# An adaLN block on one core: the start of the k projection rearranged in depth blocks

## The chip, the cores and the metric

The kernel runs on one core of a Trainium2 chip. The metric is the device time of one execution in microseconds (us). Five queues of instructions run beside each other and each keeps its order: TensorE (PE, with its weight loads PEld), VectorE (DVE), ScalarE (ACT), GpSimd (POOL) and SyncE (SP), which issues the transfers. They wait for each other through semaphores.

## The reference

One sequence of 2048 tokens of width 512 goes through two halves, each modulated by a condition vector `c`. All arrays are fp32.

```python
mod = (silu(c) @ w_mod).reshape(1, 6, 1, 512)
sa, ca, ga, sb, cb, gb = mod[:, 0], ..., mod[:, 5]
h = layernorm(x) * (1 + ca) + sa
q, k, v = split(h @ wqkv)                # 32 heads of 16
pq, pk = phi(q), phi(k)                  # phi(t) = where(t > 0, t + 1, exp(t)) + 1e-6
kv = einsum("bhsd,bhse->bhde", pk, v)
z = einsum("bhsd->bhd", pk)
o = einsum("bhqd,bhde->bhqe", pq, kv) / (einsum("bhqd,bhd->bhq", pq, z) + 1e-6)
x = x + ga * (o @ wo)
h = layernorm(x) * (1 + cb) + sb
x = x + gb * (((h @ w_gate) * (h @ w_up)) @ w_down)      # inner width 1376
```

## The kernel before

The tokens are worked in four chunks of 512, each of four token tiles of 128 (`NT` = 16 tiles, `i` counts them). The width of 512 is four depth blocks of 128. Products keep fp32 accuracy by splitting each operand into a high part, rounded for TensorE, and a low remainder: ScalarE copies the high part (`split`, L183), VectorE subtracts (L184), and TensorE makes three matmuls (high by high, high by low, low by high; `product`, L192). One such triple is needed per depth block and token tile.

The order of the work is written out by hand; no scheduler changes it. Each engine takes its instructions in the order in which the Python lines emit them. There are two pools of four PSUM banks each, `ps_acc` (`acc_bank()`) and `ps_w` (`bank()`); a new tile takes a bank that is free and waits for the last reader of it. All large SBUF tiles come from one ring of 99.

The start, L341 to L389, which the change rewrites, does the following.

- `keep_on(n)` (L141) makes TensorE multiply a tile of zeros n times. Nothing reads the result.
- `Norm` (L214) holds one chunk: `stats` (VectorE, mean and variance), `rstd_of` (a small add on VectorE and a power on GpSimd), `nmr_of` (VectorE), `xhat` (ScalarE, the normalised tile), `transpose` (TensorE, L246), and `modulated` (L259), which for one depth block scales the transposed block by column `ca` and shifts it by column `sa` on ScalarE, rounds it to the high part (VectorE when `cast` is given, otherwise a second ScalarE pass) and subtracts on VectorE.
- The columns `ca` and `sa` of the modulation are accumulated on VectorE (`mod_acc`), summed over partitions by four one-column matmuls into one bank (`mod_col`, L163) and copied out by VectorE in one instruction (`col_out`, L169).
- The weights of k are split one block at a time (`split_raw`), in turn with `modulated` of the same block.
- Token tiles 0 and 1 are then projected together, block by block (`product2`, L200), into two accumulating banks; tiles 2 and 3 follow one after the other (`proj`, L282).
- The second chunk is normalised meanwhile: its statistics for four tiles, one power, then `xhat` on ScalarE.

Phi of k is computed by `k_phi` (two ScalarE passes and one VectorE pass) and split by `k_split` (kh on ScalarE, kl on VectorE); the normalised tile is split by `k_split_x`. `t_tile` multiplies the two into four banks that accumulate over all 16 tiles. The loop over the tiles (L421) mixes for each tile `i`: the projection of tile `i + 2`, the splits of tile `i + 1`, the transposes and scalings of the next chunk in its first two tiles, `k_phi` of tile `i + 2`, and `t_tile(i)`. The dictionary `extra` (L405) adds other work behind a tile: the four splits of the q weights stand behind tiles 0, 1 and 2. `q_at` (L419) puts the first q projection at tile 3.

Of the kernel before, what the change touches and what calls it, by code (L numbers as in the profile page):

```python
# [22 lines left out]
def tile_adaln_block(  # L23
# [12 lines left out]
    nc = tc.nc  # L36
# [3 lines left out]
    KD = D // P  # L40
    NJ = 4
    CH = NJ * P
    NCH = S // CH
# [16 lines left out]
    consts = pool("consts", 1)  # L60
# [10 lines left out]
    def T(p, tag, shape=(P, D), dt=F32, bufs=None):  # L71
        cnt[0] += 1
        return p.tile(list(shape), dt, tag="t" if p is tiles else tag, name=f"{tag}_{cnt[0]}", bufs=bufs)

    def B(tag, shape=(P, D), dt=F32):

        return T(tiles, tag, shape, dt)

    def acc_bank():
        return T(ps_acc, "acc")  # L80

    def bank():
        return T(ps_w, "bank")
# [6 lines left out]
    ones = consts.tile([P, P], F32, name="ones")  # L90
# [28 lines left out]
    def load_qkv(n):  # L119
        return [load(wqkv_v[k, :, n * D:(n + 1) * D], "raw") for k in range(KD)]  # L120
# [6 lines left out]
    raw_k = load_qkv(1)  # L127
    xts.append(load_x(1))
    raw_q = load_qkv(0)
    raw_v = load_qkv(2)  # L130
# [10 lines left out]
    def keep_on(n):  # L141
        for _ in range(n):
            nc.tensor.matmul(ps_idle, idle[:, :P], idle, start=True, stop=True)
# [19 lines left out]
    def mod_col(acc, ps):  # L163

        for b in range(KD):
            nc.tensor.matmul(ps[:, b:b + 1], acc[:, b * P:(b + 1) * P], ones[:, 0:1], start=True, stop=True)
        return ps

    def col_out(v, ps, add):  # L169
        t = consts.tile([P, KD], F32, name=f"col{v}")  # L170
        nc.vector.tensor_scalar(t, ps[:, :KD], add, None, op0=ALU.add)
        return t
# [9 lines left out]
    def split(src, h, l, low=None):  # L182
        nc.scalar.activation(h, src, AF.Copy)  # L183
        (low or nc.vector).tensor_tensor(l, src, f32(h), op=ALU.subtract)  # L184

    def split_raw(raw, shape=(P, D), low=None):
        h = B("w", shape, F32R)
        l = B("w", shape, F32R)
        split(raw, h[:raw.shape[0]], l[:raw.shape[0]], low)
        return h, l  # L190

    def product(ps, pairs):  # L192

        n = len(pairs)
        for i, ((ah, al), (bh, bl)) in enumerate(pairs):
            nc.tensor.matmul(ps, ah, bh, start=i == 0, stop=False)  # L196
            nc.tensor.matmul(ps, ah, bl, start=False, stop=False)  # L197
            nc.tensor.matmul(ps, al, bh, start=False, stop=i == n - 1)  # L198

    def product2(pss, pairs):  # L200

        n = len(pairs[0])
        for i in range(n):
            for ps, p in zip(pss, pairs):
                (ah, al), (bh, bl) = p[i]
                nc.tensor.matmul(ps, ah, bh, start=i == 0, stop=False)
                nc.tensor.matmul(ps, ah, bl, start=False, stop=False)
                nc.tensor.matmul(ps, al, bh, start=False, stop=i == n - 1)

    def cut(pair, a, b):  # L210
        return pair[0][:, a:b], pair[1][:, a:b]


    class Norm:  # L214
# [25 lines left out]
        def xhat(self, *js):  # L240
            for j in js:
                self.n[j] = B("n")
                nc.scalar.activation(self.n[j], self.tiles[j], AF.Identity,  # L243
                                     scale=self.rstd[:, j:j + 1], bias=self.nmr[:, j:j + 1])

        def transpose(self, *ks):  # L246
            for k in ks:
                ps = turn_bank[0]()
                for j in range(NJ):
                    nc.tensor.transpose(ps[:, j * P:(j + 1) * P], self.n[j][:, k * P:(k + 1) * P], ident)  # L250
                self.ps[k] = ps
# [63 lines left out]
    def k_split(i):  # L315
        h, l = B("kh", dt=F32R), B("kl", dt=F32R)
        phi = phk[i]
        nc.scalar.activation(h, phi, AF.Identity, bias=eps_phi)
        nc.vector.scalar_tensor_tensor(l, phi, EPS_PHI, f32(h), op0=ALU.add, op1=ALU.subtract)
        kx[i] += [h, l]  # L320

    def t_tile(i, *ks):
        xh, xl, kh, kl = kx[i]
        first, last = i == 0, i == NT - 1
        for k in ks:
            a, b = k * P, (k + 1) * P
            nc.tensor.matmul(tacc[k], xh[:, a:b], kh, start=first, stop=False)  # L327
            nc.tensor.matmul(tacc[k], xl[:, a:b], kh, start=False, stop=False)  # L328
            nc.tensor.matmul(tacc[k], xh[:, a:b], kl, start=False, stop=last)  # L329
# [11 lines left out]
    n0 = norm[0]  # L341
    acc_ca, acc_sa = B("f"), B("f")
# [20 lines left out]
    mod_acc(acc_sa, raw_sa, [0, 1, 2, 3])  # L363
    ca = col_out(1, ps_ca, 1.0)
    keep_on(4)
    ps_sa = mod_col(acc_sa, acc_bank())
    keep_on(9)
    wk.append(split_raw(raw_k[0]))
    sa = col_out(0, ps_sa, 0.0)
    nx = Norm(xts[1])  # L370
    nx.stats(0)
    n0.modulated(ca, sa, 0, cast=nc.vector)
    wk.append(split_raw(raw_k[1]))
    n0.modulated(ca, sa, 1, cast=nc.vector)
    wk.append(split_raw(raw_k[2]))
    n0.modulated(ca, sa, 2)
    nx.stats(1)
    wk.append(split_raw(raw_k[3]))
    n0.modulated(ca, sa, 3)
    ps0, ps1 = acc_bank(), acc_bank()  # L380
    product2((ps0, ps1), [[(cut(n0.t[k], j * P, (j + 1) * P), wk[k]) for k in range(KD)] for j in range(2)])
    nx.stats(2, 3)
    nx.rstd_of()
    k_split_x(0)
    k_phi(0, ps0)
    nx.nmr_of()
    k_phi(1, ps1)
    k_split(0)
    nx.xhat(0, 1)  # L389

    tacc = [acc_bank() for _ in range(KD)]
    rows, cols = {}, {}
# [7 lines left out]
    def mod_part(v, *ks):  # L400
        if 0 in ks:
            accs[v] = B("f")
        mod_acc(accs[v], raw_m[v], ks)

    extra = {0: lambda: (wq.extend(split_raw(r) for r in raw_q[0:1]),),  # L405
             1: lambda: (wq.extend(split_raw(r) for r in raw_q[1:2]),),
             2: lambda: (wq.extend(split_raw(r) for r in raw_q[2:4]),),
             4: lambda: (wv.extend(split_raw(r) for r in raw_v[0:1]),),
             5: lambda: (wv.extend(split_raw(r) for r in raw_v[1:2]),),
             6: lambda: (wv.extend(split_raw(r) for r in raw_v[2:3]), mod_load(2),),  # L410
             7: lambda: (wv.extend(split_raw(r) for r in raw_v[3:4]),),
# [5 lines left out]
             13: lambda: (mod_part(5, 0, 1, 2), cols.update({4: col_out(4, mod_col(accs[4], bank()), 1.0)})),  # L417
             14: lambda: (mod_part(5, 3), wo_s.extend(split_raw(x) for x in raw_o)), 15: lambda: rows.update({5: mod_row(5, accs[5])})}
    q_at = {3: 0, 4: 1, 6: 2, 7: 3}  # L419
    ahead = {2: proj(2, wk)}  # L420
    for i in range(NT):  # L421
        ch, j = divmod(i, NJ)
        more = ch + 1 < NCH
        if i == 0:
            ahead[3] = proj(3, wk)
        elif i > 1:
            ahead[i + 2] = proj(i + 2, wk) if i + 2 < NT else proj(i + 6 - NT, wq)
        if i in q_at:
            qps = proj(q_at[i], wq)
        if more and j == 0:  # L430
            nx.xhat(2)
        if i + 1 < NT:
            k_split_x(i + 1)
        if more and j == 0:
            nx.xhat(3)
        if i + 1 < NT:
            k_split(i + 1)
        if more and j < 2:
            t_tile(i, 0, 1)
            nx.transpose(2 * j, 2 * j + 1)  # L440
            nx.modulated(ca, sa, 2 * j, 2 * j + 1, cast=nc.vector)
            norm[ch + 1:] = [nx]
        if ch + 2 < NCH and j == 2:
            nx2 = Norm(xts[ch + 2])
            nx2.stats(0, 1)
        if ch + 2 < NCH and j == 3:
            nx = nx2
            nx.stats(2, 3)
            nx.rstd_of()
            nx.nmr_of()  # L450
            nx.xhat(0, 1)
        if i + 2 < NT:
            k_phi(i + 2, ahead.pop(i + 2))
        else:
# [12 lines left out]
        t_tile(i, *range(2 if more and j < 2 else 0, KD))  # L467
        if i in extra:
            extra[i]()
    ga, gb, sb, cb = rows[2], rows[5], cols[3], cols[4]  # L470
# [60 lines left out]
    ps = proj(6, wq)  # L531
# [12 lines left out]
    for g in range(KD):  # L544
        a, b = g * P, (g + 1) * P
# [4 lines left out]
    ps = proj(8, wq)  # L550
# [9 lines left out]
    ps = proj(9, wq)  # L560
# [460 lines left out]
    ps = proj(11, wq)  # L1021
# [176 lines left out]
```

## Time and profile before

| | us |
|---|---|
| median of 3 runs (lowest to highest) | 570.78 (569.49 to 571.22) |
| profiled execution, device time | 570.02 |
| its span, first to last instruction | 568.3 |
| first useful k product starts | 18.03 |
| first product of tile 2's projection | 24.26 |
| first matmul of `t_tile(0)` | 29.71 |
| transposes of the third chunk start | 58.00 |

All times inside the execution count from the start of the span. A row of the timeline gives start, duration, engine, line, operation, output and inputs, shape and count; in square brackets stands how long the engine was idle before it and what ended the idle time. Matmuls are pipelined: the drawn durations overlap, and the pace is read from start to start. A row with x8 covers eight records.

### The profile page before, as it was taken

What the parts mean: (1) busy time and instruction counts of PE and PEld (TensorE: products, weight loads), DVE (VectorE), ACT (ScalarE), POOL (GpSimd) and SP (SyncE); (2) the same over time, 40 slices, a digit from 0 to 9 for tenths busy, and PEclk for the clock granted to TensorE, in tenths of its full rate; (3) what the DMA queues carried; (4) which work ended last, traced back from release to release, by engine and by line L of the source; (5) the groups of instructions that cost most, each with busy time, mean ns of one, the idle gap of its engine ahead of it and who ended that gap; (6) DMA issues with size and microseconds to landing.
All of it is one profiled execution on the core that took longest, in us unless ns stands there. A gap on an engine that the chain in (4) does not pass through costs nothing.

```text
span 568.3 us, 7356 instructions
## 1 busy us (share of the span) xinstructions
PE 560.3 (99%) x2575; PEld 458.8 (81%) x2575; DVE 373.1 (66%) x614; ACT 279.8 (49%) x500; POOL 186.2 (33%) x191
## 2 busy tenths in 40 slices
PE   8999999999999999999989999999999999999997
PEld 6778888888888878878878888787888888888886
DVE  7876868868768876759767777745554434344445
ACT  3785857546456546445865545534333333334110
POOL 2000000000011300000579666665667446556200
PEclk9999999999999999999999999999999999999999
DMA  8900223302301000804208553599336012200004
GB/s 289 374 3 2 74 75 110 114 0 62 93 0 47 29 1 37 260 0 149 57 2 277 180 190 104 202 348 330 115 111 178 26 57 55 57 19 2 0 1 148
DMA packets 50309, 59.34 MB, mean 104 GB/s; under 512 B 6432, under 2 KB 27168, under 8 KB 50272
## 3 DMA queue, kind: packets, MB, share of 16 engines
q1 hardware_dynamic: 50272, 58.87, 32.1%
q8 instruction: 20, 0.33, 0.2%
q14 instruction: 17, 0.14, 0.1%
HBM read 43.12 MB, written 15.73 MB: 104 GB/s over the span
## 4 chain that ended last, share of the span: by engine, by line
PE 89%; DMA 3%; issue 2%; POOL 1%; DVE 1%; ACT 1%; SPq 1%; POOLq 0%; ACTq 0%
PE bank L838 28%; PE acc L914 6%; PE acc L915 6%; PE acc L916 6%; PE acc L614 6%; PE bank L198 5%; PE bank L196 5%; PE bank L197 5%; PE acc L329 3%; PE acc L327 3%; PE acc L328 3%; PE bank L693 2%; PE bank L691 2%; PE bank L692 2%; PE bank L250 2%
## 5 line engine op out<-in xcount | busy, mean ns | idle before, releaser
L838 PE MATMUL bank<-h,w 128*128 128x512 f32 (+1 forms) x798 | 185.5, 390 | 1.8 <-ACT bank L843 1.2
L838 PEld LDWEIGHTS bank<-h,w 128*128 128x128 f32 (+1 forms) x798 | 148.2, 186 | 35.3 <-ACT bank L843 1.7
L843 ACT ACTIVATE bank<-bank 128x512 f32<-128x512 f32 (+1 forms) x38 | 22.1, 583 | 144.8 <-PE bank L838 144.8
L678 DVE TENSOR_TENSOR x<-acc,x 128x512 f32<-128x512 f32 (+1 forms) x73 | 49.1, 684 | 49.0 <-PE acc L916 48.2
L824 POOL TENSOR_TENSOR w<-raw,w 128x256 fp32r<-128x256 f32 (+3 forms) x38 | 42.4, 1117 | 106.4 <-ACT w L817 86.4
L184 POOL TENSOR_TENSOR w<-raw,w 128x512 fp32r<-128x512 f32 (+1 forms) x25 | 34.9, 1399 | 116.0 <-DVE mv L226 87.6
L914 PE MATMUL acc<-w,kh 128*128 128x512 f32 (+2 forms) x154 | 59.6, 387 | 0.0
L915 PE MATMUL acc<-w,kh 128*128 128x512 f32 (+2 forms) x154 | 59.6, 387 | 0.0
L916 PE MATMUL acc<-w,kl 128*128 128x512 f32 (+2 forms) x154 | 59.5, 386 | 0.0
L234 POOL TENSOR_TENSOR rstd<-ve,half 128x4 f32<-128x4 f32 (+1 forms) x9 | 9.4, 1044 | 126.0 <-DVE ve L233 124.5
L184 DVE TENSOR_TENSOR kl<-u,kh 128x512 fp32r<-128x512 f32 (+1 forms) x38 | 26.8, 746 | 33.1 <-ACT kh L183 31.2
L824 POOL TENSOR_TENSOR w<-t,w 128x512 fp32r<-128x512 f32 (+1 forms) x38 | 48.4, 1293 | 0.0
L196 PE MATMUL bank<-w,h 128*128 128x512 f32 x112 | 45.0, 402 | 0.0
L198 PE MATMUL bank<-w,h 128*128 128x512 f32 x112 | 43.9, 392 | 0.0
L197 PE MATMUL bank<-w,h 128*128 128x512 f32 x112 | 43.6, 389 | 0.0
L614 PE MATMUL acc<-w,xh 128*128 128x512 f32 x120 | 38.1, 399 | 0.0
L914 PEld LDWEIGHTS acc<-w,kh 128*128 128x128 f32 (+1 forms) x154 | 28.9, 188 | 6.0
L916 PEld LDWEIGHTS acc<-w,kl 128*128 128x128 f32 (+1 forms) x154 | 28.9, 188 | 5.9
L915 PEld LDWEIGHTS acc<-w,kh 128*128 128x128 f32 (+1 forms) x154 | 28.9, 188 | 5.9
L893 DVE TENSOR_TENSOR u<-bank,u 128x512 f32<-128x512 f32 (+1 forms) x19 | 13.1, 690 | 30.0 <-PE bank L838 30.0
L243 ACT ACTIVATE n<-x,nmr,rstd 128x512 f32<-128x512 f32 x32 | 24.1, 804 | 17.2 <-DVE nmr L237 15.9
L262 ACT ACTIVATE f<-bank,col,col 128x512 f32<-128x512 f32 x28 | 20.7, 775 | 14.5 <-PE bank L250 12.4
(177 smaller groups left out, 1105.1 us busy)
## 6 DMA issues: line engine op xcount, KB each, us to landing
raw<-in_w_mod_dram SPq DMA_DIRECT2D x24, 256.0 KB, 3.7
raw<-in_B_w_down_dram SPq DMA_DIRECT2D x20, 256.0 KB, 2.9
raw<-in_B_w_gate_dram SPq DMA_DIRECT2D x36, 128.0 KB, 3.7
raw<-in_B_w_up_dram SPq DMA_DIRECT2D x36, 128.0 KB, 3.6
x<-in_A_x_dram SPq DMA_DIRECT2D x16, 256.0 KB, 5.4
kept<-f SPq DMA_DIRECT2D x16, 256.0 KB, 2.0
f<-kept SPq DMA_DIRECT2D x16, 256.0 KB, 4.8
side_s<-h SPq DMA_DIRECT2D x16, 256.0 KB, 2.6
```

What stands on the lines that cost most here:

```text
L184: (low or nc.vector).tensor_tensor(l, src, f32(h), op=ALU.subtract)
L196: nc.tensor.matmul(ps, ah, bh, start=i == 0, stop=False)
L197: nc.tensor.matmul(ps, ah, bl, start=False, stop=False)
L198: nc.tensor.matmul(ps, al, bh, start=False, stop=i == n - 1)
L243: nc.scalar.activation(self.n[j], self.tiles[j], AF.Identity, scale=self.rstd[:, j:j + 1], bias=self.nmr[:, j:j + 1])
L614: nc.tensor.matmul(yps[i], x, y, start=False, stop=k == KD - 1 and x is al, skip_group_check=True)
L678: nc.vector.tensor_tensor(xt[:, a:b], dn[j][:, a:b], xt[:, a:b], op=ALU.add)
L824: sub = lambda out, x, y: (on or nc.gpsimd).tensor_tensor(out, x, f32(y), op=ALU.subtract)
L838: mm = lambda x, y, **kw: nc.tensor.matmul(ps, x[:, k], y, skip_group_check=True, **kw)
L914: nc.tensor.matmul(ps, hh[:, a:b], dh[:n, c:d], start=i == 0, stop=False)
L915: nc.tensor.matmul(ps, hh[:, a:b], dl[:n, c:d], start=False, stop=False)
L916: nc.tensor.matmul(ps, hl[:, a:b], dh[:n, c:d], start=False, stop=i == len(hs) - 1)
```

## The change

Six things are rewritten, all between the modulation columns and token tile 3.

1. The four one-column matmuls of `sa` write two banks: the first column has a bank of its own, the other three share one. VectorE copies each column out by itself; the copy of the first stands before the first weight split's subtraction, the other three behind the first block's scaling.
2. `keep_on(9)` behind them becomes `keep_on(2)`, and `keep_on(4)` stays.
3. All four token tiles of the first chunk are projected per depth block (`k_block`) into four banks, for blocks 0 and 1. Blocks 2 and 3 follow tile by tile. `product2` goes. All four blocks are rounded on VectorE.
4. The second chunk's statistics and power are done in two halves of two tiles; `xhat` of its tiles 2 and 3 is done on VectorE in one instruction each (`xhat_on`), tiles 0 and 1 stay on ScalarE. The statistics of its first tile stand behind the scaling of block 2.
5. `k_split_x(1)`, `k_phi(1)` and `k_split(1)` stand before the loop. In the loop, the transposes and scalings of the second chunk stand at tiles 1 and 2 (before: 0 and 1), and at tile 2 they come first; `t_tile(2)` goes before the projection of tile 4.
6. The four splits of the q weights stand behind the last scaling of the second chunk, at tile 2.

```diff
-    ps_sa = mod_col(acc_sa, acc_bank())
-    keep_on(9)
-    wk.append(split_raw(raw_k[0]))
-    sa = col_out(0, ps_sa, 0.0)
+    ps_sa = [acc_bank()]
+    ps_sa += [acc_bank()] * (KD - 1)
+    sa = consts.tile([P, KD], F32, name="col0")
+    def sa_block(b):
+        nc.tensor.matmul(ps_sa[b][:, b:b + 1], acc_sa[:, b * P:(b + 1) * P], ones[:, 0:1], start=True, stop=True)
+    def sa_out(b):
+        nc.vector.tensor_scalar(sa[:, b:b + 1], ps_sa[b][:, b:b + 1], 0.0, None, op0=ALU.add)
+    def block_in(b):
+        n0.modulated(ca, sa, b, cast=nc.vector)
+    def w_in(b):
+        wk.append(split_raw(raw_k[b]))
+    for b in range(KD):
+        sa_block(b)
+    keep_on(2)
+    k_ps = [acc_bank(), acc_bank(), bank(), bank()]
+    def k_block(b, *js):
+        for j in js:
+            (hh, hl), (wh, wl) = cut(n0.t[b], j * P, (j + 1) * P), wk[b]
+            nc.tensor.matmul(k_ps[j], hh, wh, start=b == 0, stop=False)
+            nc.tensor.matmul(k_ps[j], hh, wl, start=False, stop=False)
+            nc.tensor.matmul(k_ps[j], hl, wh, start=False, stop=b == KD - 1)
+    sa_out(0)
+    w_in(0)
+    block_in(0)
+    for b in range(1, KD):
+        sa_out(b)
+    w_in(1)
+    block_in(1)
+    k_block(0, 0, 1, 2, 3)
     nx = Norm(xts[1])
+    w_in(2)
+    block_in(2)
     nx.stats(0)
-    n0.modulated(ca, sa, 0, cast=nc.vector)
-    wk.append(split_raw(raw_k[1]))
-    n0.modulated(ca, sa, 1, cast=nc.vector)
-    wk.append(split_raw(raw_k[2]))
-    n0.modulated(ca, sa, 2)
+    k_block(1, 0, 1, 2, 3)
+    w_in(3)
+    block_in(3)
     nx.stats(1)
-    wk.append(split_raw(raw_k[3]))
-    n0.modulated(ca, sa, 3)
-    ps0, ps1 = acc_bank(), acc_bank()
-    product2((ps0, ps1), [[(cut(n0.t[k], j * P, (j + 1) * P), wk[k]) for k in range(KD)] for j in range(2)])
-    nx.stats(2, 3)
-    nx.rstd_of()
+    nx.rstd_of(0, 2)
     k_split_x(0)
-    k_phi(0, ps0)
-    nx.nmr_of()
-    k_phi(1, ps1)
+    k_block(2, 0)
+    k_block(3, 0)
+    k_phi(0, k_ps[0])
+    nx.nmr_of(0, 2)
+    nx.stats(2)
     k_split(0)
+    nx.stats(3)
+    nx.rstd_of(2, 4)
+    k_block(2, 1)
+    k_block(3, 1)
+    k_split_x(1)
+    k_phi(1, k_ps[1])
     nx.xhat(0, 1)
+    nx.xhat_on(nc.vector, 2)
+    k_split(1)
+    nx.xhat_on(nc.vector, 3)
+    k_block(2, 2)
+    k_block(3, 2)
+    k_block(2, 3)
+    k_block(3, 3)
...
+        def xhat_on(self, engine, *js):
+            for j in js:
+                self.n[j] = B("n")
+                engine.tensor_scalar(self.n[j], self.tiles[j], self.mv[:, j, 0:1], self.rstd[:, j:j + 1],
+                                     op0=ALU.subtract, op1=ALU.mult)
...
+    turn_at = {4 * ch + j: (ch + 1, 2 * j, 2 * j + 1) for ch in range(1, NCH - 1) for j in range(2)}
+    turn_at.update({1: (1, 0, 1), 2: (1, 2, 3)})
     for i in range(NT):
...
+        if i == 2:
+            turn_x()
+            wq.extend(split_raw(r) for r in raw_q)
...
+        if i in turn_at and i != 2:
             t_tile(i, 0, 1)
+            done = 2
+            turn_x()
+        if i == 2:
+            t_tile(i, *range(KD))
+            done = KD
+            ahead[i + 2] = proj(i + 2, wk)
```

More of the change, by code (lines that the diff above doesn't have):

```diff
@@ L198, in product @@
             nc.tensor.matmul(ps, al, bh, start=False, stop=i == n - 1)
[L200 to L208, printed above, removed]
     def cut(pair, a, b):
@@ L403, in mod_part @@
         mod_acc(accs[v], raw_m[v], ks)
[L405 to L408, printed above, removed]
+    extra = {4: lambda: (wv.extend(split_raw(r) for r in raw_v[0:1]),),
              5: lambda: (wv.extend(split_raw(r) for r in raw_v[1:2]),),
@@ L419, in tile_adaln_block @@
     q_at = {3: 0, 4: 1, 6: 2, 7: 3}
-    ahead = {2: proj(2, wk)}
+    ahead = {2: k_ps[2], 3: k_ps[3]}
+    turn_at = {4 * ch + j: (ch + 1, 2 * j, 2 * j + 1) for ch in range(1, NCH - 1) for j in range(2)}
+    turn_at.update({1: (1, 0, 1), 2: (1, 2, 3)})
     for i in range(NT):
         ch, j = divmod(i, NJ)
[L423 to L426, printed above, removed]
+        done = 0
+        if i > 2:
             ahead[i + 2] = proj(i + 2, wk) if i + 2 < NT else proj(i + 6 - NT, wq)
@@ L429, in tile_adaln_block, with turn_x @@
             qps = proj(q_at[i], wq)
-        if more and j == 0:
+        def turn_x():
+            to, *ks = turn_at[i]
+            nx.transpose(*ks)
+            nx.modulated(ca, sa, *ks, cast=nc.vector)
+            norm[to:] = [nx]
+        fresh = i > 0 and ch + 1 < NCH and j == 0
+        if i == 2:
+            turn_x()
+            wq.extend(split_raw(r) for r in raw_q)
+        if fresh:
             nx.xhat(2)
-        if i + 1 < NT:
+        if 0 < i < NT - 1:
             k_split_x(i + 1)
-        if more and j == 0:
+        if fresh:
             nx.xhat(3)
-        if i + 1 < NT:
+        if 0 < i < NT - 1:
             k_split(i + 1)
-        if more and j < 2:
+        if i in turn_at and i != 2:
             t_tile(i, 0, 1)
-            nx.transpose(2 * j, 2 * j + 1)
-            nx.modulated(ca, sa, 2 * j, 2 * j + 1, cast=nc.vector)
-            norm[ch + 1:] = [nx]
+            done = 2
[4 more added lines that the diff above has]
+            ahead[i + 2] = proj(i + 2, wk)
         if ch + 2 < NCH and j == 2:
@@ L466, in tile_adaln_block @@
             nc.scalar.activation(zb, zps, AF.Identity, bias=eps_z)
-        t_tile(i, *range(2 if more and j < 2 else 0, KD))
+        t_tile(i, *range(done, KD))
         if i in extra:
```

## The prediction

> **What bounds the kernel now.** I read the page first, for who carries the span.
>
> ```profile
> span 568.3 us, 7356 instructions
> PE 560.3 (99%) x2575; PEld 458.8 (81%) x2575; DVE 373.1 (66%) x614; ACT 279.8 (49%) x500; POOL 186.2 (33%) x191
> PE 89%; DMA 3%; issue 2%; POOL 1%; DVE 1%; ACT 1%; SPq 1%; POOLq 0%; ACTq 0%
> ```
>
> TensorE is busy for 99% and is 89% of the chain that ended last. A change that neither adds nor removes useful matmuls can then win only where TensorE stands still or does filler. Next the stretches (start and end, length, then busy time and count of PE, PEld, DVE, ACT and POOL), to see where that is.
>
> ```profile
> 0.00:18.03 18.03, 15.53 (x70) 12.44 (x71) 13.09 (x32) 6.86 (x10) 3.52 (x15) 1.00 0.88 310
> 18.03:50.00 31.97, 31.86 (x144) 25.09 (x143) 27.80 (x55) 23.39 (x39) 1.38 (x1) 1.00 0.34 122
> 50.00:155.00 105.00, 105.00 (x506) 87.12 (x506) 79.51 (x137) 62.35 (x104) 2.01 (x2) 1.00 0.24 71
> 155.00:264.00 109.00, 109.00 (x530) 89.00 (x529) 83.22 (x143) 60.79 (x104) 11.96 (x9) 1.00 0.17 58
> ```
>
> From 50 to 264 us TensorE never rests, so what the front gains there is carried on, and the change moves nothing behind token tile 3: after it each engine's instructions stand in the same order. What follows 264 us I take to shift along, its loads being released by the work before them. The busy column hides short pauses, because a paused matmul is drawn longer; so I read single rows of TensorE, start and duration.
>
> ```profile
> 14.94 1.05 PE L166 MATMUL acc<-ones,f 128*128 128x1 f32 x8
> 15.85 2.34 PE L143 MATMUL acc<-w 128*128 128x512 f32 x9
> 18.03 0.39 PE L206 MATMUL acc<-w,h 128*128 128x512 f32 x1
> ...
> 24.26 0.40 PE L196 MATMUL bank<-w,h 128*128 128x512 f32 x1
> ...
> 29.71 0.39 PE L327 MATMUL acc<-kh,xh 128*128 128x512 f32 x1
> ...
> 36.98 0.40 PE L196 MATMUL bank<-w,h 128*128 128x512 f32 x1
> ...
> 40.27 0.39 PE L327 MATMUL acc<-kh,xh 128*128 128x512 f32 x1
> ...
> 58.00 1.04 PE L250 MATMUL bank<-ident,n 128*128 128x128 f32 x8
> ```
>
> From 24.26 to 29.71 run the 24 matmuls of tiles 2 and 3: 5.45 us, so 0.227 us each when fed. That is the ruler. The 24 of the paired tiles 0 and 1 take 18.03 to 24.26, 6.23 us: 0.78 is pause. The 12 of tile 4's projection take 36.98 to 40.27, 3.29 against 2.72: 0.57 is pause. The nine before 18.03 are filler. In the printed chain, transfers precede 19.87; but VectorE has no idle time there (rows below, back to back), so it is that queue and not a load that is late.
>
> **The change, part by part.** The feeders' rows, VectorE first:
>
> ```profile
> 16.03 0.16 DVE L171 TENSOR_SCALAR col<-acc 128x4 f32<-128x4 f32 x1 [0.47 <-PE acc L166]
> 16.34 0.70 DVE L225 BATCH_NORM_STATS2 st<-x 128x6 f32<-128x512 f32 x1
> 17.07 0.18 DVE L226 BATCH_NORM_AGGREGATE mv<-st 128x2 f32<-128x6 f32 x1
> 17.17 0.40 DVE L270 CAST h<-f 128x512 fp32r<-128x512 f32 x1
> ...
> 18.21 0.69 DVE L184 TENSOR_TENSOR w<-raw,w 128x512 fp32r<-128x512 f32 x1
> 18.81 0.42 DVE L270 CAST h<-f 128x512 fp32r<-128x512 f32 x1
> 19.26 0.69 DVE L273 TENSOR_TENSOR h<-f,h 128x512 fp32r<-128x512 f32 x1
> 19.87 0.69 DVE L184 TENSOR_TENSOR w<-raw,w 128x512 fp32r<-128x512 f32 x1
> ```
>
> ```profile
> 13.64 0.63 ACT L183 ACTIVATE w<-raw 128x512 fp32r<-128x512 f32 x1 [1.49 <-DMA raw<-in_A_wqkv_dram]
> ...
> 16.23 0.78 ACT L262 ACTIVATE f<-bank,col,col 128x512 f32<-128x512 f32 x1 [1.96 <-DVE col L171]
> ...
> 23.76 0.60 ACT L291 ACTIVATE phi<-acc 128x512 f32<-128x512 f32 x1 [1.33 <-PE acc L208]
> 24.39 0.64 ACT L292 ACTIVATE phi<-phi 128x512 f32<-128x512 f32 x1
> ...
> 25.51 0.68 DVE L295 SCALAR_TENSOR_TENSOR phi<-acc,phi 128x512 f32<-128x512 f32 x1
> ...
> 26.23 0.72 ACT L318 ACTIVATE kh<-phi,eps_phi 128x512 fp32r<-128x512 f32 x1
> ```
>
> *First column.* The four columns took eight records in 1.05 us. With a bank of its own, column 0 is complete after two records, about 15.3. Its copy (0.16) ends at 15.5 instead of 16.19, ScalarE scales until 16.3 (0.78), and the cast follows at 16.37, because the statistics that stood before it (16.34 to 17.25) have moved behind block 2. It ends at 16.77, so the first product starts at 16.8 instead of 18.03: **1.2 us won**. Seven of thirteen fillers go; they covered a wait and cost nothing now. The other three copies add 0.1 us each to VectorE.
>
> *Four tiles per block.* VectorE needs per block 0.60 (weight remainder), 0.45 (cast) and 0.61 (remainder), start to start: 1.66 us. Two tiles give TensorE 6 x 0.227 = 1.36 us per block, so it ran dry; four give 2.72. The 0.78 pause goes. In its place: the third matmul wants the remainder of block 0, which runs 16.82 to 17.5, at 17.25: 0.3 lost. Block 1 is ready at 19.7 (cast 18.6) and wanted from 19.8. Block 2 is ready at 21.4, wanted 22.5. With statistics (0.8) ahead of it, block 3 is ready at 23.8, and its remainder is wanted at 23.7: 0.1 lost. The fourth tile's bank is the one block 1 is scaled from; that read ends at 18.6, before 19.1. So 48 products end at 16.8 + 10.9 + 0.4 = 28.1 instead of 29.71: 1.6 ahead. Casting blocks 2 and 3 on VectorE takes 2 x 0.45 more there.
>
> *Phi and tile 1.* Tile 0's sum is complete at 24.2, and its chain (0.60, 0.64, 0.68, 0.72) is done by 27, ahead of 28.1. Late next is tile 1's: ScalarE's copy from 26.9, two phi steps, then the two xhat put before kh (0.80 each, row below), and kh (0.72). That is 0.63 + 0.60 + 0.64 + 1.60 + 0.72 = 4.2; neighbours in a queue overlap by 0.09 (18.21 + 0.69 against 18.81), so kh ends at 30.7 and kl (0.69) at 31.45. TensorE, at tile 1 from 30.8, wants it at 31.25: 0.2 lost.
>
> *Second chunk in halves, q weights last.* Two xhat move from ScalarE to VectorE; no row of before is this form, nearest is the product with one column:
>
> ```profile
> 11.37 0.75 DVE L161 SCALAR_TENSOR_TENSOR f<-raw,sc,f 128x512 f32<-128x512 f32 x1
> 12.04 0.48 DVE L159 TENSOR_SCALAR f<-raw,sc 128x512 f32<-128x512 f32 x1
> ```
>
> It is between 0.48 and 0.75 each; I take 0.48, as one tensor is read. The power on GpSimd goes from one call to two, idle cover on both sides. The last scalings now stand before the q splits, and the 12 matmuls of tile 2's product before tile 4's projection: 2.72 us of cover, so the 0.57 pause goes. The q splits (four of 0.60) now stand ahead of tile 3's remainders and of the next statistics; TensorE meanwhile has tile 4, 5 and q 0, 36 x 0.227 = 8.2 us. By then TensorE is 1.6 - 0.2 + 0.57 = 1.97 ahead. SP's loads keep order and count, so no transfer is moved.
>
> *What it meets next.* The third chunk's transposes at 58.00. Their last input and the queue that leads to it:
>
> ```profile
> 26.49 0.16 DVE L237 SCALAR_TENSOR_TENSOR nmr<-mv,rstd 128x4 f32<-128x4 f32 x1 [0.30 <-POOL rstd L234]
> ...
> 29.62 0.69 DVE L184 TENSOR_TENSOR xl<-n,xh 128x512 fp32r<-128x512 f32 x1 [1.77 <-ACT xh L183]
> ...
> 30.94 0.69 DVE L319 SCALAR_TENSOR_TENSOR kl<-phi,kh 128x512 fp32r<-128x512 f32 x1 [0.62 <-ACT kh L318]
> ...
> 32.53 0.43 DVE L270 CAST h<-f 128x512 fp32r<-128x512 f32 x1 [0.90 <-ACT f L262]
> ...
> 51.12 0.16 DVE L237 SCALAR_TENSOR_TENSOR nmr<-mv,rstd 128x4 f32<-128x4 f32 x1 [1.21 <-POOL rstd L234]
> ...
> 56.26 0.80 ACT L243 ACTIVATE n<-x,nmr,rstd 128x512 f32<-128x512 f32 x1
> ```
>
> The last xhat ends at 57.06; the transpose that reads it is the fourth of eight, about 58.3: 1.2 us of slack. VectorE's queue sets that xhat through nmr at 51.12. It starts 0.7 earlier and gets 2.25 us more work (casts 0.9, xhat 0.96, small ones 0.4), but of its 3.59 us of idle time (0.30 + 1.77 + 0.62 + 0.90) my walk leaves 1.6 (0.3, 0.2, 0.4, 0.4, 0.3 before casts, phi and kl): -0.7 + 2.25 - 3.59 + 1.6 = about 0.45 earlier. So TensorE may come 1.2 + 0.45 = 1.65, say **1.7 us**, earlier and not 1.97; the rest turns into a pause there. Behind it nothing changes order.
>
> **Sum.** The profiled execution took 570.02 us; less 1.7 that is 568.3. The median of the runs is 570.78, which gives 569.1. I predict the middle, 568.7. Ends: with no new pause 1.2 + 0.78 + 0.57 = 2.55 won, 567.5; if the third chunk's queue comes no earlier, 1.2 won, 568.8 to 569.6.
>
> **Rivals.** *Slower: VectorE's added work.* If VectorE idles as long as before (3.59), its queue ends 2.25 - 0.7 = 1.55 later; the slack of 1.2 doesn't cover it, and the transposes wait: 0.35 slower, 570.4 (571.1 from the median). It decides once idle time stays above 3.2 us. For it: 27.80 of 31.97 us busy already. Against: three of the four waits quoted are for ScalarE, which loses two casts and two xhat.
>
> *The column doesn't come early.* If its copy still waits for all four, the start is 0.7 later, as is the whole front: 1.0 won, 569.0 to 569.8. In the built program the semaphore stands on the first column's matmul, which speaks against.
>
> *The clock falls back.* Fewer fillers stand between 13 and 16.8 us. The trace knows a slow matmul:
>
> ```profile
> 4.71 1.91 PE L143 MATMUL acc<-w 128*128 128x512 f32 x4
> ...
> 8.01 1.32 PE L143 MATMUL acc<-w 128*128 128x512 f32 x5
> ```
>
> Four took 1.91 us, five then 1.32: over 0.4 us each, then 0.23. If the half pace returned for the six us that it lasted at first (1.99 to about 8), three us are lost: 570.02 - 1.7 + 3.0 = 571.3, or 572.1 from the median; it decides at 3.4 us of half pace. Against: the new gap is 0.3 us, and the idle time before the transposes at 10.08 did not bring it back.
>
> ```profile
> 10.08 0.66 PE L257 MATMUL bank<-ident,n 128*128 128x128 f32 x4 [0.52 <-ACT n L243]
> ```
>
> The Trainium skill's page "TensorE: Matmul & The Clock Gate" (Part 1, "What's actually happening") halves the clock only after a window of about 3.4 us without activity. By that rule the change would cost nothing here; the trace agrees as far as 0.52 us of idling goes.
>
> **Chances.** Forecast (1.3 to 2.5 won; 567.5 to 569.5) 0.68, of it 0.50 at 1.7 or more, as the ends lie 0.4 below and 0.85 above; queue no earlier, or no early column, 0.15; VectorE's work on the path 0.10; clock 0.07. About 0.3%, 1.7 us, is what a measurement can tell from no change. VectorE's and the clock's price stay inside it and pass it only when exceeded (half pace for over 6.8 us; xhat at 0.75 and the q splits late as well): 0.05 of each. So faster 0.50; within 0.18 + 0.15 + 0.05 + 0.02 = 0.40; slower 0.10. Range 567.3 to 571.0: it reaches to VectorE's price and leaves out what exceeds it and the clock.
>
> **What would show it.** First product near 16.8; no pause over 0.3 until 28.1; a pause of 0.1 to 0.4 at tile 1's kl and at the third chunk's transposes near 56.4; tile 4's projection in 2.72 us. Wrong: matmuls 0.4 apart after 16.8, or a pause over 1.5 us at the transposes.

## The result and the profile after

The changed kernel takes 567.6 us (median of 6 runs, 567.43 to 568.24); the kernel before took 570.0 us beside it (6 runs, 569.49 to 571.22). The ratio is 0.9957, 95% interval 0.9945 to 0.9969: faster by 2.4 us, 0.43%. The profiled executions, 568.24 and 570.02 us, lie 1.8 us apart.

The page of the changed kernel: span, busy times, and the chain that ended last, by engine.

```profile
span 566.5 us, 7353 instructions
PE 556.8 (98%) x2568; PEld 456.7 (81%) x2568; DVE 375.1 (66%) x622; ACT 277.0 (49%) x496; POOL 186.5 (33%) x192
PE 90%; issue 2%; ACT 2%; DMA 2%; POOL 1%; DVE 1%; SPq 1%; POOLq 0%; DVEq 0%
```

TensorE has 7 instructions fewer, the fillers, and is still what carries the span. Single rows of TensorE show where the time went; compare the prediction's rows at 18.03, 29.71, 36.98 and 58.00.

```profile
15.03 1.05 PE L367 MATMUL acc<-ones,f 128*128 128x1 f32 x8
...
17.03 0.47 PE L386 MATMUL acc<-w,h 128*128 128x512 f32 x1 [0.38 <-DVE h L266]
...
18.00 0.40 PE L386 MATMUL acc<-w,h 128*128 128x512 f32 x1
...
28.31 0.39 PE L323 MATMUL acc<-kh,xh 128*128 128x512 f32 x1
...
31.29 0.40 PE L324 MATMUL acc<-kh,xl 128*128 128x512 f32 x1
31.63 0.50 PE L325 MATMUL acc<-kl,xh 128*128 128x512 f32 x1
31.96 0.39 PE L323 MATMUL acc<-kh,xh 128*128 128x512 f32 x1
...
38.55 0.39 PE L196 MATMUL bank<-w,h 128*128 128x512 f32 x1
...
41.27 0.39 PE L196 MATMUL bank<-w,h 128*128 128x512 f32 x1
...
56.24 1.14 PE L246 MATMUL bank<-ident,n 128*128 128x128 f32 x8
57.14 0.48 PE L323 MATMUL acc<-kh,xh 128*128 128x512 f32 x1
```

The first product starts 1.00 us earlier than before, the 48 products of four tiles end 1.40 us earlier (28.31 against 29.71), tile 4's projection runs through in 2.72 us, and at the third chunk's transposes TensorE is 1.76 us ahead. They take 0.90 us to the next matmul. In the kernel before they took 0.79, which this row of it gives against 58.00:

```profile
58.79 0.47 PE L327 MATMUL acc<-kh,xh 128*128 128x512 f32 x1
```

So 0.11 us of the lead is lost there and 1.65 stays.

Places count from the start of the span, which isn't fixed to the work. The one-column matmuls of `sa` start at 15.03 here, at 14.94 in the kernel before, and between 14.60 and 15.16 in the traces below, though nothing ahead of them that they wait for was changed. For differences of tenths of a us the distance from this row is the safer measure. By it the lead is 1.09 us at the first product and 1.74 behind the transposes.

Now the changed kernel's rows of VectorE and ScalarE that feed these points.

```profile
15.45 0.16 DVE L370 TENSOR_SCALAR col<-acc 128x1 f32<-128x1 f32 x1 [0.40 <-PE acc L367]
...
16.45 0.43 DVE L266 CAST h<-f 128x512 fp32r<-128x512 f32 x1 [0.24 <-ACT f L258]
...
21.26 0.69 DVE L215 BATCH_NORM_STATS2 st<-x 128x6 f32<-128x512 f32 x1
...
30.09 0.55 DVE L239 TENSOR_SCALAR n<-x,mv,rstd 128x512 f32<-128x512 f32 x1
30.88 0.69 DVE L315 SCALAR_TENSOR_TENSOR kl<-phi,kh 128x512 fp32r<-128x512 f32 x1 [0.25 <-ACT kh L314]
...
50.61 0.16 DVE L227 SCALAR_TENSOR_TENSOR nmr<-mv,rstd 128x4 f32<-128x4 f32 x1 [1.21 <-POOL rstd L224]
...
50.81 1.52 ACT L233 ACTIVATE n<-x,nmr,rstd 128x512 f32<-128x512 f32 x2 [4.27 <-DVE nmr L227]
```

Two numbers matter for what follows. `nmr` of the third chunk starts at 50.61 instead of 51.12, and the first matmul behind the transposes starts 6.53 us after it. ScalarE, which normalises that chunk, has then waited 4.27 us for `nmr`.

### The profile page after: what moved, and what is told of

The parts are those of the page before. It is cut to its first block, busy times and chain, and to the rows that moved or that the text cites. A ratio compares the mean times of both kernels' runs of the same rounds, so it can differ in the third digit from the quotient of the medians.

```text
span 566.5 us, 7353 instructions
## 1 busy us (share of the span) xinstructions
PE 556.8 (98%) x2568; PEld 456.7 (81%) x2568; DVE 375.1 (66%) x622; ACT 277.0 (49%) x496; POOL 186.5 (33%) x192
## 4 chain that ended last, share of the span: by engine, by line
PE 90%; issue 2%; ACT 2%; DMA 2%; POOL 1%; DVE 1%; SPq 1%; POOLq 0%; DVEq 0%
PE bank L886 27%; PE acc L962 6%; PE acc L963 6%; PE acc L964 6%; PE acc L662 6%; PE bank L196 5%; PE bank L197 5%; PE bank L198 5%; PE acc L325 3%; PE acc L324 3%; PE acc L323 3%; PE bank L741 2%; PE bank L739 2%; PE bank L740 2%; PE bank L246 2%
## 5 line engine op out<-in xcount | busy, mean ns | idle before, releaser
L196 PE MATMUL bank<-w,h 128*128 128x512 f32 x104 | 41.7, 401 | 0.0
L198 PE MATMUL bank<-w,h 128*128 128x512 f32 x104 | 40.6, 390 | 0.0
L197 PE MATMUL bank<-w,h 128*128 128x512 f32 x104 | 40.5, 389 | 0.0
L233 ACT ACTIVATE n<-x,nmr,rstd 128x512 f32<-128x512 f32 x30 | 22.6, 804 | 16.0 <-DVE nmr L227 14.7
L183 ACT ACTIVATE w<-raw 128x512 fp32r<-128x512 f32 (+2 forms) x44 | 26.2, 618 | 2.5 <-DMA raw<-in_A_wqkv_dram 1.5
```

## The experiments

Each kernel was timed beside the kernel before; "won" is the median of before less the kernel's own. Medians are known to about 0.7 us (the half-width of the intervals), so smaller steps are read in the traces. Every kernel below computes the whole reference.

### The changed kernel once more

> The changed kernel, unaltered, for a second trace. Theory (TensorE's feed at the start sets the gain): against the kernel before, 1.8 us less, as in the two traces (568.3 to 566.5); first product within 0.2 of 17.03, third chunk's transposes within 0.2 of 56.24. Rival (something behind the front adds to it, since the medians differ by 2.4 and the traces by 1.8): transposes at the same place, but the stretch from 57.1 to the end over 0.4 us shorter than its 509.4.

567.96 us (567.43 to 568.67, 5 runs), 2.5 won, ratio 0.9959 (0.9946 to 0.9971). The rows of the transposes and of the last matmul, from this trace:

```profile
56.03 1.17 PE L246 MATMUL bank<-ident,n 128*128 128x128 f32 x8
...
561.84 0.28 PE L964 MATMUL acc<-w,kl 128*128 128x256 f32 x1
```

and the last matmul of the changed kernel's first trace:

```profile
562.64 0.28 PE L964 MATMUL acc<-w,kl 128*128 128x256 f32 x1
```

The two traces of one and the same kernel are 0.2 us apart at the transposes and 0.8 at the end. The 0.2 is there at the columns already (14.82 against 15.03). From the matmul behind the transposes to the end of the span this trace takes 508.7 us and the first 509.4; that difference is the sign that the rival named. But the other traces of this document take 508.7 to 509.5 there, and one 510.5, with no edit in that stretch, and the first trace is the slowest of its six executions. So whether the 0.6 us by which the traces fall short of the medians is scatter or a gain behind the front stays open.

### Two tiles per block again

```diff
-    k_block(0, 0, 1, 2, 3)
+    k_block(0, 0, 1)
...
-    k_block(1, 0, 1, 2, 3)
+    k_block(1, 0, 1)
...
-    k_block(2, 2)
-    k_block(3, 2)
-    k_block(2, 3)
-    k_block(3, 3)
+    for j in (2, 3):
+        for b in range(KD):
+            k_block(b, j)
```

> Undoes the third part alone: blocks 0 to 3 for tiles 0 and 1 only, then tile 2, then tile 3. Theory (VectorE's pace per block sets TensorE's): tile 0's last block is ready at 23.1 (cast) and 23.8 (remainder) as before, so tile 0 ends at 24.4 as in the changed kernel, but with 12 fewer matmuls done; the 12 cost 2.7 us later, less what pauses at tile 1 and the transposes took (0.2): 2.0 to 2.6 us over the changed kernel, about the time of the kernel before. Rival (only the 0.78 us pause of the kernel before comes back): 0.8 us over.

570.3 us (569.64 to 571.35, 11 runs), 0.2 won, ratio 1.0001 (0.9992 to 1.001). Rows of TensorE:

```profile
17.16 0.47 PE L386 MATMUL acc<-w,h 128*128 128x512 f32 x1 [0.38 <-DVE h L266]
...
23.28 0.50 PE L386 MATMUL acc<-w,h 128*128 128x512 f32 x1 [1.25 <-DVE h L266]
...
25.73 0.39 PE L386 MATMUL bank<-w,h 128*128 128x512 f32 x1
...
58.83 1.03 PE L246 MATMUL bank<-ident,n 128*128 128x128 f32 x8
```

Without the four tiles everything else of the change wins nothing. The 24 matmuls of tiles 0 and 1 take 8.57 us (17.16 to 25.73), so 3.12 us are pause, against 0.78 before; at block 3 TensorE stands still for 1.25 us at a stretch. VectorE needs more time per block here: from the first cast to the start of the last block's remainder its rows span 6.68 us (16.58 to 23.26) instead of 5.32 (17.17 to 22.49), and two casts of 0.45 us are the main thing that was added between them. The transposes begin 2.6 us later than in the changed kernel.

### The first column late again

Three runs take the early column apart. The first puts all four columns into one bank with one copy:

```diff
-    ps_sa = [acc_bank()]
-    ps_sa += [acc_bank()] * (KD - 1)
+    ps_sa = [acc_bank()] * KD
...
-    sa_out(0)
+    nc.vector.tensor_scalar(sa, ps_sa[0][:, :KD], 0.0, None, op0=ALU.add)
...
-    for b in range(1, KD):
-        sa_out(b)
```

> Undoes the first part alone: the four columns of sa in one bank, one copy. Theory: the copy starts about 0.7 later (after all eight records, 16.1 instead of 15.45), so do the first product (17.7) and the third chunk's transposes (56.9), because VectorE's queue starts later by the same; the time is 0.6 to 0.7 over the changed kernel. Rival (VectorE's queue to the transposes has slack and catches up): first product at 17.7, transposes within 0.3 of 56.24, under 0.3 us lost.

568.95 us (567.89 to 570.09, 9 runs), 1.5 won, ratio 0.9975 (0.9964 to 0.9986).

```profile
17.63 0.50 PE L385 MATMUL acc<-w,h 128*128 128x512 f32 x1 [0.95 <-DVE h L266]
...
56.85 1.16 PE L246 MATMUL bank<-ident,n 128*128 128x128 f32 x8
```

The first product is 0.60 us later than in the changed kernel's trace, the transposes 0.61, both within 0.1 us of what was foretold. But the executions fall into two groups: six with a mean granted clock of 0.999 or 1.000 took 567.89 to 569.19, median 568.3, and three with 0.997 took 569.60 to 570.09. Lateness and clock are mixed here. So a second run fills the wait:

```diff
-    keep_on(2)
+    keep_on(6)
     k_ps = [acc_bank(), acc_bank(), bank(), bank()]
```

> The four columns in one bank with one copy for all of them, as in the run of that edit, and six fillers instead of two behind the columns, so that TensorE isn't idle while the column is late. Theory (a late column costs 0.6 to 0.8 us by itself, and what that run lost beyond it in three of its nine executions came from the clock): no execution below a mean clock of 0.999, 568.4 to 568.6 and a spread under 1.3 us. Rival (the late column costs about 0.2 us, the clock did the rest): 567.9 to 568.1. Rival (the third chunk's transposes wait in both, the column is free): as the changed kernel, 567.7.

568.21 us (567.89 to 569.09, 5 runs), 2.65 won, ratio 0.9959 (0.9947 to 0.9972), and no execution below a clock of 0.999.

```profile
57.72 0.48 PE L323 MATMUL acc<-kh,xh 128*128 128x512 f32 x1
```

That agrees with the clock part of the theory, but weakly: at three in nine, none in five would come about one time in eight. In the trace the late column costs 0.58 us (57.72 against 57.14), just under what was expected. In the time it can't be seen: 568.21 lies below the 568.4 to 568.6 foretold, and 2.65 won is no less than the change itself wins, as the rivals had it. What a late column costs by itself is therefore known from traces alone.

The third run leaves the column early and puts the old number of fillers ahead of the products:

```diff
-    keep_on(2)
+    keep_on(9)
     k_ps = [acc_bank(), acc_bank(), bank(), bank()]
```

> Undoes the second part alone: nine fillers before the first product instead of two. Theory: they end at 15.94 + 2.1, so the first product is at about 18.1; the pause of 0.1 at the third matmul and some small ones go, so 0.7 to 1.0 us over the changed kernel. Rival (the fillers keep the clock up and cost nothing): no later end, as the products at 17 to 20 were at half pace without them.

568.81 us (568.13 to 569.03, 6 runs), 1.7 won, ratio 0.9971 (0.9959 to 0.9982).

```profile
14.73 1.05 PE L367 MATMUL acc<-ones,f 128*128 128x1 f32 x8
...
17.82 0.39 PE L386 MATMUL acc<-w,h 128*128 128x512 f32 x1
...
57.57 0.47 PE L323 MATMUL acc<-kh,xh 128*128 128x512 f32 x1
```

The early column is worth something only if the fillers go with it. Counted from the columns, which come early in this trace (14.73 against 15.03), the first product starts 1.09 us later than in the changed kernel's, and 0.73 of it is left behind the transposes. That is the 0.7 to 1.0 foretold, and the time has 0.8.

### All four xhat on ScalarE

```diff
-    nx.xhat_on(nc.vector, 2)
+    nx.nmr_of(2, 4)
+    nx.xhat(2)
     k_split(1)
-    nx.xhat_on(nc.vector, 3)
+    nx.xhat(3)
```

> Undoes the move of xhat alone: the second chunk's tiles 2 and 3 normalised on ScalarE, one before and one after the second k split. Theory: kh of tile 1 stands behind one more xhat (0.71), so TensorE waits about 0.8 at tile 1's product instead of 0.1, and the third chunk's transposes come 0.7 to 1.2 later; 0.7 to 1.4 us over the changed kernel. Rival (VectorE's queue is what limits, and it is relieved of 1.1 us): within 0.3 us of the changed kernel or faster.

569.58 us (569.0 to 571.64, 12 runs), 1.0 won, ratio 0.9985 (0.9976 to 0.9993). Rows of VectorE and TensorE:

```profile
51.93 0.16 DVE L227 SCALAR_TENSOR_TENSOR nmr<-mv,rstd 128x4 f32<-128x4 f32 x1 [1.21 <-POOL rstd L224]
```

```profile
31.53 0.50 PE L323 MATMUL acc<-kh,xh 128*128 128x512 f32 x1 [0.54 <-ACT kh L314]
...
57.93 0.77 PE L246 MATMUL bank<-ident,n 128*128 128x128 f32 x5 [0.59 <-ACT n L233]
58.45 0.47 PE L323 MATMUL acc<-kh,xh 128*128 128x512 f32 x1
```

1.5 us less is won than with the change, a little over the 0.7 to 1.4 that was expected; the trace has 1.31 (58.45 against 57.14), or 1.55 counted from the columns. Where it goes is as expected: TensorE stands 0.54 us for `kh` at tile 1's product, `nmr` comes 1.32 us later, and the transposes wait for the last xhat in the middle of their group. The trace also shows what holds VectorE's queue back: it waits 1.50 us for `kh` of tile 1 (to 31.50) and 1.16 for phi of tile 2 (to 33.36), both behind ScalarE's two extra passes. In the changed kernel the first wait is 0.25 us and the second isn't there.

### The q splits where they were

```diff
-            wq.extend(split_raw(r) for r in raw_q)
...
-    extra = {4: lambda: (wv.extend(split_raw(r) for r in raw_v[0:1]),),
+    extra = {0: lambda: (wq.extend(split_raw(r) for r in raw_q[0:1]),),
+             1: lambda: (wq.extend(split_raw(r) for r in raw_q[1:2]),),
+             2: lambda: (wq.extend(split_raw(r) for r in raw_q[2:4]),),
+             4: lambda: (wv.extend(split_raw(r) for r in raw_v[0:1]),),
```

> Undoes the last part alone: the q splits behind tiles 0, 1 and 2, the rest as changed. Theory: they stand ahead of the second chunk's last scalings on both engines, so tile 4's projection pauses again for 0.3 to 0.6, but the third chunk's transposes, which VectorE's queue sets, absorb it: 0 to 0.3 us over the changed kernel. Rival (the 0.57 us pause was a gain of its own): 0.5 us over.

567.78 us (567.49 to 569.24, 6 runs), 2.8 won, ratio 0.9955 (0.9943 to 0.9967).

```profile
38.56 0.39 PE L196 MATMUL bank<-w,h 128*128 128x512 f32 x1
...
41.24 0.50 PE L198 MATMUL bank<-w,h 128*128 128x512 f32 x1
41.58 0.40 PE L196 MATMUL bank<-w,h 128*128 128x512 f32 x1
...
57.42 0.48 PE L323 MATMUL acc<-kh,xh 128*128 128x512 f32 x1
```

No loss can be measured. But the trace shows the pause that the theory named: tile 4's projection takes 3.02 us (38.56 to 41.58) instead of 2.72, the 0.30 at its last matmuls, and TensorE passes the third chunk's transposes 0.28 us later than in the changed kernel. So the place of the q splits accounts for a part of the 0.57 us at tile 4. The next run looks at the other candidate.

### Tile 4's projection ahead of tile 2's product

```diff
-            t_tile(i, *range(KD))
-            done = KD
-            ahead[i + 2] = proj(i + 2, wk)
+            ahead[i + 2] = proj(i + 2, wk)
+            t_tile(i, *range(KD))
+            done = KD
```

> The changed kernel with one order turned round: tile 4's projection stands ahead of tile 2's product again, as before the change, on TensorE alone. Theory (the 12 matmuls of cover are what removed the pause, and in the changed kernel's trace VectorE writes the last remainder at 39.28 to 39.97 with phi's steps between the scalings): the projection starts near 35.8 and its last matmul can't start before 39.97, so it takes about 4.4 us instead of 2.72; 1.6 us of pause, of which the 0.11 us that TensorE waits at the third chunk's transposes anyway is absorbed: 1.5 us over the changed kernel, near 569.3. Rival A (the prediction's own size): the pause is the old 0.57 us, 0.45 us over, 568.2. Rival B: VectorE is early enough and no pause comes, 567.8.

569.84 us (569.21 to 572.02, 11 runs), 1.0 won, ratio 0.9987 (0.9976 to 0.9999).

```profile
35.57 0.48 PE L196 MATMUL bank<-w,h 128*128 128x512 f32 x1
...
38.09 0.50 PE L196 MATMUL bank<-w,h 128*128 128x512 f32 x1 [0.90 <-DVE h L266]
...
40.22 0.40 PE L323 MATMUL acc<-kh,xh 128*128 128x512 f32 x1
...
58.72 0.48 PE L323 MATMUL acc<-kh,xh 128*128 128x512 f32 x1
```

The projection takes 4.65 us instead of 2.72 and the transposes are passed 1.58 us later, near the theory's 1.5 and not the old pause of 0.57. So the 12 matmuls of tile 2's product are the cover for the last scalings. They cover more than the pause that was there before; the last 0.30 us need the q splits out of the way as well.

### The fillers and the clock

In the changed kernel without any filler behind the `ca` columns (they compute nothing that is read):

```diff
-    keep_on(4)
...
-    keep_on(2)
     k_ps = [acc_bank(), acc_bank(), bank(), bank()]
```

> All six fillers between the two groups of one-column matmuls and the first product left out. Theory: TensorE waits for VectorE there anyway; no change within 0.2 us. Rival (the clock needs them): products from 17 on at 0.43 instead of 0.227 for some us, 1.5 us or more over the changed kernel.

569.44 us (568.66 to 570.67, 8 runs), 1.1 won, ratio 0.9979 (0.9968 to 0.9989). My theory was wrong here and its rival right, if just short of its 1.5 us: 1.4 less is won than with the change. Every one of the eight executions has a mean clock of 0.994 to 0.997.

```profile
14.60 1.05 PE L366 MATMUL acc<-ones,f 128*128 128x1 f32 x8 [0.93 <-DVE f L161]
16.59 0.47 PE L384 MATMUL acc<-w,h 128*128 128x512 f32 x1 [0.94 <-DVE h L266]
...
17.80 0.59 PE L385 MATMUL acc<-w,h 128*128 128x512 f32 x1
...
21.17 0.43 PE L384 MATMUL acc<-w,h 128*128 128x512 f32 x1
```

Its stretches (start and end, length, busy time and count of PE, PEld, DVE, ACT, POOL, then granted clock, DMA share, GB/s):

```profile
12.00:17.00 5.00, 3.12 (x25) 2.77 (x23) 4.22 (x9) 1.93 (x3) 0.00 (x0) 1.00 1.05 389
17.00:20.00 3.00, 3.00 (x10) 2.21 (x9) 2.85 (x9) 2.72 (x5) 0.00 (x0) 0.64 1.04 384
```

From 17.80 to 21.17 eight matmuls start in 3.37 us, 0.42 each; at 0.227 they would take 1.82. That is 1.55 us lost, behind two gaps of under 1 us that leave TensorE busy for 3.12 of 5 us. Half the clock for 3.37 us lowers the mean over the span of 567.7 us by 0.003, so a mean of 0.997 is read here as one such spell. The same stretch of the changed kernel has 4.64 and the full clock:

```profile
12.00:17.00 5.00, 4.64 (x32) 3.69 (x31) 4.22 (x10) 2.17 (x4) 0.00 (x0) 1.00 1.05 387
```

The counterpart is the kernel before with two fillers in place of nine and nothing else changed:

```diff
-    keep_on(9)
+    keep_on(2)
```

> The kernel before with two fillers in place of nine, and nothing else. Theory: the first product starts at 17.7, but VectorE's rows after it are unmoved (third and fourth block remainders end at 22.6 and 23.2), so the paired tiles end when they did and the time is that of the kernel before within 0.2. Rival (the fillers cost the kernel their share): 0.3 to 1.1 us under the kernel before.

570.91 us (569.82 to 572.2, 11 runs), ratio 1.0005 (0.9996 to 1.0015). Four executions at clock 1.000 took 569.82 to 570.80, seven at 0.996 or 0.997 took 570.38 to 572.20. Rows of its trace:

```profile
17.79 0.79 PE L206 MATMUL acc<-w,h 128*128 128x512 f32 x1 [1.05 <-DVE h L270]
18.37 0.63 PE L207 MATMUL acc<-w,h 128*128 128x512 f32 x1
```

The median is 0.36 us over that of before, a little outside the theory's 0.2. The four executions with the clock kept have a median of 570.5, that of the kernel before: nothing is gained by taking fillers away from a start that waits for the column anyway. The trace, of one of the seven, has the half pace right behind a gap of 1.05 us.

### What the traces say together

TensorE passes the third chunk's transposes at the later of two times: when it gets there itself, or 6.5 us after VectorE's `nmr`. Start of the one-column matmuls of `sa`, start of `nmr`, start of the matmul behind the transposes, and two distances, from rows of the kind shown above:

| kernel | columns | nmr | next matmul | from columns | from nmr | which is later |
|---|---|---|---|---|---|---|
| before | 14.94 | 51.12 | 58.79 | 43.85 | 7.67 | TensorE |
| changed | 15.03 | 50.61 | 57.14 | 42.11 | 6.53 | nmr |
| changed, once more | 14.82 | 50.44 | 56.96 | 42.14 | 6.52 | nmr |
| one bank | 15.05 | 51.24 | 57.77 | 42.72 | 6.53 | nmr |
| one bank, six fillers | 14.97 | 51.19 | 57.72 | 42.75 | 6.53 | nmr |
| nine fillers | 14.73 | 51.05 | 57.57 | 42.84 | 6.52 | nmr |
| all xhat on ScalarE | 14.79 | 51.93 | 58.45 | 43.66 | 6.52 | nmr |
| no fillers | 14.60 | 51.71 | 58.25 | 43.65 | 6.54 | nmr |
| q splits where they were | 15.04 | 50.62 | 57.42 | 42.38 | 6.80 | TensorE |
| projection first | 14.87 | 50.47 | 58.72 | 43.85 | 8.25 | TensorE |
| two tiles per block | 15.16 | 52.88 | 59.62 | 44.46 | 6.74 | TensorE |

So in the traces the late column, the extra fillers and ScalarE's xhat cost at this point just what they delay VectorE's queue, whatever they do to the first product. Counted from the columns, the loss against the changed kernel agrees with the times for two tiles per block (2.35 us; 2.3 less won), projection first (1.74; 1.5), all xhat on ScalarE (1.55; 1.5), no fillers (1.54; 1.4) and nine fillers (0.73; 0.8). The late column's 0.6 and the q splits' 0.27 are in the traces only. The changed kernel is balanced to 0.11 us between the two; none of the variants run here beats it by more than can be measured, and a further gain at this point needs both to come earlier.

## Why the prediction was right

The forecast of 568.7 us is 1.1 over the measured median. Of this, 0.4 is the base: the prediction started halfway between 570.02 and 570.78, and the kernel before then had a median of 570.0. The other 0.7 is the size: 2.4 us won and not 1.7. That the profiled execution took 568.24, beside 570.02 less 1.7 = 568.3, is partly luck, as it was the slowest of six.

- **First column.** Forecast start of the first product 16.8, found 17.03: 1.0 won and not 1.2. Of the 0.23 missing, 0.09 is the later start of the one-column matmuls in this trace (15.03 against 14.94), and the rest is the step from cast to matmul: I took the cast's end as the start, and the trace has 0.58 us between the two starts (16.45 to 17.03) where the cast lasts 0.43. What it is worth further on is set by VectorE's queue and not by the first product; that is 0.6 us in the traces and isn't seen in the time.
- **Four tiles per block.** Forecast: 48 products end at 28.1; found 28.31. From start to end that is 11.28 us, 0.38 over the pace, where the forecast had 0.4. Of it, 0.29 goes in the first three steps (17.03 to 18.00, where 0.68 is the pace), at the remainder that was named. Taking this part back costs 2.3 us, the largest loss of any run here, and its price is not the old pause of 0.78 but 3.12 us. The prediction counted the added casts in VectorE's queue and not on the path, because of the longer cover of four tiles; the run shows what the start costs without that cover.
- **Tile 1's kl.** Forecast 31.45 for its end and 0.2 lost; found 31.57 (30.88 and 0.69) and 0.21 lost (31.29 to 31.96 is 0.67 us for two matmuls, fed ones take 0.45).
- **Tile 4's projection.** Forecast 2.72 us, found 2.72. Both reasons given were needed: without the cover of tile 2's product the pause is 1.93 us, without the q splits behind the scalings it is 0.30.
- **xhat on VectorE.** Taken at 0.48 us between 0.48 and 0.75; found 0.55 and 0.54.
- **The cap at the transposes.** The prediction let TensorE come no more than 1.65 us earlier, because `nmr` would come 0.45 earlier. Found: 0.51 earlier, 1.65 us kept, and a pause of 0.11 instead of 0.27, as TensorE arrived a little later than forecast. This was the step that decided the number, and the table shows the same cap in seven traces. But the 0.45 itself came out by luck. VectorE's rows from the first cast to `nmr`, before and after (start and end, length, busy time and count):

```profile
17.17:51.12 33.95, 28.63 (x58) 1.00 0.34 125
16.45:50.61 34.16, 31.66 (x66) 1.00 0.36 133
```

The work added is 3.03 us and not 2.25. The prediction started its queue 0.7 us earlier because the statistics pass at 16.34 had moved behind block 2, and left out that this pass (about 0.8 us, now at 21.26) then lies inside the stretch. The idle time falls by 2.82 us (5.32 to 2.50) and not by 1.99. The two errors of 0.8 us cancel.
- **The size.** The terms that the prediction names add up to what the traces have at the transposes, 1.65 to 1.74 us, and the medians lie 2.4 us apart. The difference arises behind 57 us, where two traces of the changed kernel differ by as much, so it can't be put down to a step.

Of the rivals, *VectorE's added work* didn't come: its queue was 0.51 us earlier, not 1.55 later. It was nearer than its price says: with the idle time of before, 3.03 us of added work would have made the queue 2.3 us later. *The column doesn't come early* was refuted by the copy at 15.45. *The clock falls back* didn't happen in the changed kernel, whose eleven executions are at a mean clock of 0.999 or 1.000, but the argument I had against it was too weak. I gave it 0.07 on the strength of a 0.52 us gap that did no harm. With no filler behind the `ca` columns the mean clock was 0.997 or less in eight executions of eight, with two behind the `sa` columns of the kernel before in seven of eleven, and with the late column and two in three of nine. The change kept six of thirteen fillers and a gap of 0.38 us; without them more than half of its gain would be gone.

The Trainium skill's page "TensorE: Matmul & The Clock Gate" (Part 1, "What's actually happening") puts the fall to half rate behind at least one idle window of about 3.4 us, and the return behind a busy one of about the same length. The length of the half pace agrees with the second (17.80 to 21.17 is 3.37 us). The first does not hold here: between 12 and 22 us no gap in the two traces with the half pace is longer than 1.05 us, and the clock fell all the same. The measurement decides.

## What to carry to other kernels

When a stretch is bound by two engines in turn, find for each the point where it is last waited for, and price an edit by what it moves there: here a distance of 6.53 us from one small VectorE instruction held in seven traces to 0.01 us, while the start of the first product misled: nine fillers moved it by 1.09 us and cost 0.73, and all xhat on ScalarE left it in place and cost 1.55. Count such distances from an instruction ahead of the edit and not from the start of the span. Here TensorE, running dry in a loop of short blocks, was cured by more independent work per block, and the work moved onto the feeding engine was safe only behind that cover. A forecast that comes out right may still hold two wrong terms: compare busy and idle time separately, as for VectorE's queue above. Fillers that nothing reads may be holding the clock: take them out only as far as the wait that they cover goes too.

## What the runs showed of the hardware

TensorE's granted clock was halved for about 3.4 us behind idle gaps that were much shorter than I had expected. The trace without fillers has two, of 0.93 and 0.94 us, and all eight executions of that kernel have a mean clock of 0.997 or less. The trace of the kernel before with two fillers has one of 1.05 us, and seven of eleven executions have such a mean. A halved spell cost 1.55 us of matmul time where products were waiting.

Neither the length of a gap nor the share of busy time over 5 us decides by itself. In the first trace of the changed kernel TensorE stands idle for 1.83 us ahead of its first transposes:

```profile
10.17 0.66 PE L253 MATMUL bank<-ident,n 128*128 128x128 f32 x4 [1.83 <-ACT n L233]
```

The matmuls behind it keep the full pace: the next two fillers take 0.71 us together, as in the kernel before, though TensorE was busy for only 3.17 of the 5 us from 8 to 13. With two tiles per block there is the gap of 1.25 us, and the clock stays at 1.00 with less busy time than the 3.95 of 5 us (13 to 18) at which the kernel before with two fillers lost it:

```profile
19.00:24.00 5.00, 3.62 (x12) 1.75 (x11) 4.86 (x11) 2.52 (x5) 0.00 (x0) 1.00 1.05 388
```

Mean clocks of 0.997 and less also came up now and then elsewhere: in two of eleven executions with two tiles per block, one of twelve with all xhat on ScalarE, two of eleven with the projection first, and two of the 61 of the kernel before that were timed beside these runs; in none of the eleven of the changed kernel. No trace of these executions was kept. What sets which executions are hit isn't settled by these runs.
